# Every other hand-ordered step does one weight operation instead of two, and steps 1 to 5 have fewer filler matmuls

## The chip, the cores and the metric

The kernel runs on one core of a Trainium2 chip. The metric is the device time of one launch in microseconds (us). The engines are TensorE (PE in the rows; PEld is its weight load, which overlaps it), VectorE (DVE), ScalarE (ACT), GpSimd (POOL) and SyncE (SP, which issues most of the DMAs).

## What is computed

Two stages in float32, for 4 batches, 8 heads of 64, 768 positions, 512 model columns and 1024 inner columns:

```python
# attention: a local window of 96 keys and 8 global ones, with a slope per head
scores = q @ k.T / sqrt(64) - slope[h] * dist       # only kept keys
a = softmax(scores); x = a @ v                      # x: 768 x 512 per batch
# then a gated feed-forward layer
h = relu(x @ w_in)
c = conv_w[0]*h[t-1] + conv_w[1]*h[t] + conv_w[2]*h[t+1]
out = (h * sigmoid(c)) @ w_out
```

The weights `w_in` and `w_out` arrive as float64. They have to be brought to float32 on the core, and each is kept as two planes, a rounded high part and a low part, so that three matmuls of a faster type (high by high, high by low, low by high) give one product of float32 quality.

## The kernel before, in words

The work is cut into 8 units of 384 rows (half a batch each). Each unit has four jobs (a pair of heads each), and each job three steps of 128 rows: 96 steps in all, numbered s = 0 to 95 through the kernel. In one step TensorE multiplies scores for two heads (`scores`, L363, tile `s`), VectorE adds the distance table and takes the maxima (`maxima`, L390, two instructions, one for each head, each followed by a short read of its result), ScalarE takes exponentials into `pbuf` (`exps`, L407), TensorE transposes these (`transposes`, L432 and L434, tile `t`), ScalarE copies the result out (L437, tile `pt`), and TensorE multiplies by the values (`block`, L483, tile `pv` or `spare`). There are two score tiles in PSUM: the scores of step s can start when the exponentials of step s - 2 have read theirs. After three steps of a job its output is scaled and split into a high and a low part (`xh`, `xl`). The feed-forward layer of a unit follows: `mm1` (L521, or L542 where a slice is done early), `conv` (L567 on POOL, L568 and L569 on VectorE), gates, and `mm2` (L632).

The weights come in 16 pieces (`wr`, one DMA each, four buffers). Each piece needs four operations on VectorE and one on POOL: mask and shift (L292), sign bits (L294), low bits (L296), then POOL's copy to the high plane (L301), then the subtraction that gives the low plane (L307). That makes 64 weight operations on VectorE; eight pieces are for `w_in`, and the first four of them are all that the first half of `mm1` needs. The buffer of a piece is free for the next load after L296.

The first 14 steps are ordered by hand (`by_hand`): each engine gets its instructions in the order in which the code writes them. A step writes the scores of s, the values of s - 2, a slice of `mm1` if its weights were done early enough (`mm1_early`), a number of filler matmuls (`warm`, L152, 128x128 bf16 on zeros, into columns that nobody reads; the number stands in the table `WARM` at place s + 1), the transposes of s - 1, then the maxima and exponentials of s, and after them VectorE's other work, at the end of which stand the weight operations. A list `chores["dve"]` holds these in their order; each call of `work("dve", 0.1)` takes the next one from it. From step 14 on a scheduler places what the code hands it. There, 1.2 us of weight operations (by the program's own costs, as 0.62 for most) are handed over behind the maxima of each step until the list is empty, and each step also gets a share of `mm1`. `mm1` calls `need`, which emits any weight operation that is still missing ahead of it.

Of the kernel before, what the change touches and what calls it, by code (L numbers as in the profile page):

```python
# [40 lines left out]
HAND = 14  # L41
FREE = 4
NATIVE = 12
WARM = (64, 0, 20, 20, 16, 10, 8, 6, 6, 6, 6, 6, 6, 6, 6)
EARLY = 1
HINT = 48
DECODE_LATER = (1.2, 1.2)
# [20 lines left out]
def fast_path(tc, io):  # L68
# [81 lines left out]
    def warm(n):  # L150
        for _ in range(n):
            T.matmul(wp[:, TB:], wz, wz, start=True, stop=True)  # L152

    warm(WARM[0])

# [47 lines left out]
    def table(h, c0=0, c1=NT, X=V):  # L203
        r = slice(c0, c1)
        X.tensor_scalar(tab[:, h, r], rel[:, r], -(2.0 ** (2 - h)), 1.0, ALU.mult, ALU.mult)
# [142 lines left out]
    def free(s):  # L348
        return s < NB * FREE

    def scores(s):
        m, i = steps[s]
        b, u, hp = jobs[m]
        w = NKC[u]
        first = u == 0 and i == 0
        n = W0 if first else WIN
        k0 = key_start(u, i)
        both = ps_s.tile([P, 2, 256], F32, tag="s", name=f"s{s}")
        sp = [both[:, 0], both[:, 1]]
        for j in range(2):  # L360
            if m < NATIVE:
                rq, rk = raw[m]
                last_mm[s] = T.matmul(  # L363
                    sp[j][:, :n],
                    rq[:D, j * TB + i * P : j * TB + (i + 1) * P],
                    rk[:D, j * w + k0 : j * w + k0 + n],
                    start=True,
                    stop=True,
                )
                continue  # L370
            qh, ql, kk = qk[m]
            for n_, (q_, st, sp_) in enumerate(((qh, True, False), (ql, False, True))):
                last_mm[s] = T.matmul(  # L373
                    sp[j][:, :n],
                    q_[:, j * TB + i * P : j * TB + (i + 1) * P],
                    kk[:, j * w + k0 : j * w + k0 + n],
                    start=st,
                    stop=sp_,
                )
        st_s[s] = (sp, n, first)  # L380

    def maxima(s):
        m, i = steps[s]
        b, u, hp = jobs[m]
        sp, n, first = st_s[s]
        mm = p1.tile([P, 8], F32, tag="mm", name=f"mm{s}", bufs=6)
        for j in range(2):
            h = 2 * hp + j
            tb = tab[:, h, WIN:] if first else tab[:, h, 0:WIN]
            last_ttr[s] = V.tensor_tensor_reduce(  # L390
                out=sp[j][:, :n], in0=sp[j][:, :n], in1=tb,
                scale=-0.125, scalar=3.0e38, op0=ALU.add, op1=ALU.min,
                accum_out=mm[:, j : j + 1],
            )
        st_s[s] = (sp, n, mm)

    def exps(s):
        m, i = steps[s]
        sp, n, mm = st_s[s]
        pb = pbuf[s % NPB]  # L400
        total = mm[:, 2:4]
        if free(s):
            if i == 0:
                sums[m] = p1.tile([P, 4 * NB], F32, tag="sum", name=f"sum{m}", bufs=2)
            total = sums[m][:, 2 * i : 2 * i + 2]
        for j in range(2):
            last_exp[s] = A.activation(  # L407
                pb[:, j * WIN : j * WIN + n], sp[j][:, :n], AF.Exp,
                bias=mm[:, j : j + 1], scale=-1.0, accum_out=total[:, j : j + 1],
            )  # L410
        st_s[s] = (pb, n, mm)
        if s < SHARED and not free(s):
            A.activation(mm[:, 4:6], mm[:, 2:4], AF.Identity, bias=eps)

    def normalise(s):
        pb, n, mm = st_s[s]
        if s >= SHARED:
            V.tensor_scalar(mm[:, 4:6], mm[:, 2:4], 1.0e-9, None, ALU.add)
        V.reciprocal(mm[:, 6:8], mm[:, 4:6])  # L419
        for j in range(2):  # L420
            x, inv = pb[:, j * WIN : j * WIN + n], mm[:, 6 + j : 7 + j]
            if j and s < SHARED:
                A.activation(x, x, AF.Copy, scale=inv)
            else:
                G.tensor_scalar(x, x, inv, 1.0, ALU.mult, ALU.mult)  # L425

    def transposes(s):
        m, i = steps[s]
        pb, n, _ = st_s.pop(s)
        pt = ps_t.tile([P, 2, 2, P], F32, tag="t", name=f"t{s}")  # L430
        for j in range(2):
            T.transpose(pt[:, 0, j], pb[:, j * WIN : j * WIN + P], ident)  # L432
            if n > P:
                T.transpose(pt[:, 1, j], pb[:, j * WIN + P : j * WIN + 256], ident)  # L434
        sb = p2.tile([P, 2, 2, P], F32, tag="pt", name=f"pt{s}", bufs=NPT)
        k = 2 if n > P else 1
        last_ev[s] = A.activation(sb[:, :k], pt[:, :k], AF.Copy)  # L437
        st_pt[s] = sb
# [10 lines left out]
    def inverses(m):  # L449
        t, n = sums[m], 2 * NB  # L450
        V.tensor_scalar(t[:, n:], t[:, :n], 1.0e-9, None, ALU.add)
        V.reciprocal(t[:, n:], t[:, n:])

    def spread(m):
        for i in range(NB):
            for j in range(2):
                k = 2 * (NB + i) + j
                T.matmul(  # L458
                    wp[64 * j : 64 * j + 64, i * P : (i + 1) * P],
                    sums[m][:, k : k + 1].to_broadcast([P, D]),  # L460
                    ident, start=True, stop=True,
                )

    def factors(m):
        sums[m] = p1.tile([P, TB], F32, tag="ob", name=f"x{m}")
        A.activation(sums[m], wp[:, :TB], AF.Copy)

    def scaled(m):
        t = sums[m]
        V.tensor_tensor(t, pv[m], t, ALU.mult)  # L470
        pv[m] = t

    def block(m, i):
        if m not in pv:
            if m % 2:
                pv[m] = spare[:, :TB]
            else:
                pv[m] = ps_v.tile([P, TB], F32, tag="v", name=f"pv{m}")
        sb = st_pt.pop(NB * m + i)
        whole = jobs[m][1] == 0 and i == 0  # L480
        for c, n, q in ((0, P, 0),) if whole else ((0, P, 0), (1, NLATE, NEAR)):
            for j in range(2):
                T.matmul(  # L483
                    pv[m][64 * j : 64 * j + 64, i * P + q : (i + 1) * P],
                    vt[m][:n, i, c, 64 * j : 64 * j + 64],
                    sb[:n, c, j, q:],
                    start=c == 0,
                    stop=c == 1 or whole,
                )

    def mixed_high(m):
        xh = px.tile([P, TB], F32R, tag="xh", name=f"xh{m}")
        xl = px.tile([P, TB], F32R, tag="xl", name=f"xl{m}")
        xt[m] = (xh, xl)
        A.activation(xh, pv[m], AF.Copy)

    def mixed_low(m):
        xh, xl = xt[m]
        cur["mixed"] = V.tensor_tensor(xl, pv[m], xh.bitcast(F32), ALU.subtract)
# [5 lines left out]
    def ends(s):  # L505
        return s >= 0 and s % NB == NB - 1
# [42 lines left out]
    def mm1_early(s):  # L549
        k = begun[0]  # L550
        if k < NK - 1 and s >= 6 + NB * k and done.get((k, 0), s) < s - 1:
            for f in range(EARLY):
                mm1_slice(f, k)
            begun[0] += 1
# [167 lines left out]
    def work(eng, budget):  # L722
        q = chores[eng]
        while q and budget > 0 and q[0][0] <= cur["s"]:
            _, cost, fn, args = q.pop(0)
            fn(*args)
            budget -= cost
# [39 lines left out]
    def by_hand(s):  # L767
        m, i = steps[s]
        p, q = s - 1, s - 2
        scores(s)  # L770
        if q >= 0 and free(q):
            block(*steps[q])
        if ends(q):
            spread(q // NB)
        mm1_early(s)
        warm(WARM[s + 1])
        if ends(q):
            factors(q // NB)
        if p >= 0 and free(p):
            transposes(p)  # L780
        maxima(s)
        exps(s)
        if ends(s - 3):
            mixed_low((s - 3) // NB)
        if ends(p):
            inverses(p // NB)
        if ends(q):
            scaled(q // NB)
            mixed_high(q // NB)
        if p >= 0 and not free(p):  # L790
            normalise(p)
        if i == 0 and m + 1 < NPAIR:
            table(2 * m + 2, X=G)
            table(2 * m + 3, X=G)
        for _ in range(2 if s else 1):
            work("dve", 0.1)
        if s == HAND - 1:
            mixed_low(q // NB)
        if s == 5:
            limits()  # L800
        if s in (4, 6):
            conv_weights((s - 4) // 2)
        work("pool", 1.3)
# [276 lines left out]
```

## Time and profile before

| | |
|---|---|
| median of 3 runs | 448.04 us (446.02 to 448.59) |
| the profiled execution | 445.51 us, of which the span (first to last instruction) is 443.5 us |
| TensorE busy | 435.4 us, 98% of the span; its weight loads 378.0 us |
| VectorE, ScalarE, POOL busy | 349.3, 296.2, 208.4 us |
| DMA | 58.69 MB, 132 GB/s on average |

A busy TensorE is not a TensorE at its peak: the ends of matmuls are modelled, and neighbours overlap in the rows. The starts of neighbours tell more than the durations. The granted clock (PEclk) is 1.00 where TensorE runs at 2.4 GHz, and 0.50 at 1.2 GHz.

In the profiled execution the hand-ordered steps run from 6.6 us to 42.4 us, and the weight operations end at about 89 us. The scores of steps 14, 20, 24, 28 and 31 start at 42.36, 62.00, 74.73, 86.01 and 95.22 us.

### The profile page before, as it was taken

How to read it: one execution, taken by the hardware profiler on the slowest of the kernel's cores; microseconds unless marked ns; L12 is line 12 of the kernel's file. 1: busy time of each engine (PE TensorE's matmuls, PEld its weight loads, DVE VectorE, ACT ScalarE, POOL GpSimd, SP SyncE). 2: the span in 40 equal slices, each digit the busy share in tenths (PEclk: the TensorE clock that was granted, in tenths of full speed). 3: DMA queues.
4: the chain of work that ended last, by engine and by line, in shares of the span. 5: the costliest groups of instructions: out<-in, count | busy, mean ns of one | idle time of the engine just before them, and what ended most of it. 6: DMA issues, size and time to landing. Idle time of an engine off the chain costs nothing.

```text
span 443.5 us, 8969 instructions
## 1 busy us (share of the span) xinstructions
PE 435.4 (98%) x3044; PEld 378.0 (85%) x3044; DVE 349.3 (79%) x921; ACT 296.2 (67%) x819; POOL 208.4 (47%) x292
## 2 busy tenths in 40 slices
PE   9999999899999999999999999999999999999996
PEld 8777877689889998889989998889989998799885
DVE  5797998969989988757989898857989976657600
ACT  3566689897998775656676776656776787756511
POOL 4211644525744964546656874556656741013000
PEclk9999999999999999999999999999999999999999
DMA  7966855223144334243235334353334424970111
GB/s 216 311 205 191 251 165 168 73 84 91 64 142 143 109 109 132 77 142 117 91 133 149 105 108 126 96 138 112 108 118 141 130 85 129 333 253 0 47 50 52
DMA packets 20836, 58.69 MB, mean 132 GB/s; under 512 B 2736, under 2 KB 2992, under 8 KB 20784
## 3 DMA queue, kind: packets, MB, share of 16 engines
q1 hardware_dynamic: 16960, 51.56, 37.7%
q10 hardware_dynamic: 3824, 6.49, 4.0%
q8 instruction: 26, 0.43, 0.4%
q14 instruction: 26, 0.21, 0.1%
HBM read 51.75 MB, written 6.29 MB: 131 GB/s over the span
## 4 chain that ended last, share of the span: by engine, by line
PE 94%; DVE 3%; ACT 2%; issue 0%; POOL 0%; ACTq 0%; POOLq 0%; DVEq 0%
PE h L521 30%; PE o L632 29%; PE pv L483 8%; PE s L373 6%; PE s L363 5%; PE t L432 5%; PE t L434 4%; PE warm L152 3%; PE o L896 1%; ACT pt L437 1%; PE h L542 1%; PE spare L483 1%; PE warm L458 1%; DVE s L390 1%; DVE w L294 0%; ACT pbuf L407 0%
## 5 line engine op out<-in xcount | busy, mean ns | idle before, releaser
L425 POOL TENSOR_SCALAR pbuf<-pbuf,mm 128x232 f32<-128x232 f32 (+1 forms) x140 | 99.5, 720 | 77.8 <-DVE mm L419 58.5
L407 ACT ACTIVATE pbuf<-s,mm 128x232 f32<-128x232 f32 (+1 forms) x192 | 82.9, 441 | 45.7 <-DVE mm L390 39.3
L390 DVE CUSTOM_DVE_ANT_0 s<-s,tab 128x232 f32<-128x232 f32 (+1 forms) x192 | 73.1, 384 | 14.1 <-PE s L373 5.9
L567 POOL TENSOR_SCALAR c<-hbuf,cw 128x382 f32<-128x382 f32 (+1 forms) x64 | 49.2, 771 | 63.1 <-ACT hbuf L531 58.7
L632 PE MATMUL o<-woh,gh 128*128 128x512 f32 x184 | 75.3, 409 | 0.0
L632 PE MATMUL o<-wol,gh 128*128 128x512 f32 x184 | 73.3, 398 | 0.0
L632 PE MATMUL o<-woh,gl 128*128 128x512 f32 x184 | 72.9, 397 | 0.0
L437 ACT ACTIVATE pt<-t 128x512 f32<-128x512 f32 (+1 forms) x96 | 54.1, 564 | 18.3 <-PE t L434 16.7
L521 PE MATMUL h<-xh,wih 128*128 128x384 f32 x252 | 59.6, 349 | 0.0
L521 PE MATMUL h<-xl,wih 128*128 128x384 f32 x252 | 58.0, 343 | 0.0
L521 PE MATMUL h<-xh,wil 128*128 128x384 f32 x252 | 56.7, 345 | 0.0
L568 DVE SCALAR_TENSOR_TENSOR c<-hbuf,cw,c 128x382 f32<-128x382 f32 (+1 forms) x64 | 47.6, 750 | 10.5 <-POOL c L567 10.2
L432 PE MATMUL t<-ident,pbuf 128*128 128x128 f32 x192 | 46.4, 276 | 0.2
L521 PEld LDWEIGHTS h<-xh,wih 128*128 128x128 f32 x252 | 43.4, 190 | 3.2 <-issue 1.7
L521 PEld LDWEIGHTS h<-xh,wil 128*128 128x128 f32 x252 | 44.1, 190 | 2.0 <-issue 1.5
L521 PEld LDWEIGHTS h<-xl,wih 128*128 128x128 f32 x252 | 43.2, 189 | 1.3 <-issue 0.9
L569 DVE SCALAR_TENSOR_TENSOR c<-hbuf,cw,c 128x382 f32<-128x382 f32 (+1 forms) x64 | 43.8, 687 | 0.5
L483 PEld LDWEIGHTS pv<-pt,v 128*64 128x64 f32 (+1 forms) x664 | 34.0, 136 | 10.1 <-issue 4.1
L483 PE MATMUL pv<-pt,v 128*64 128x128 f32 (+1 forms) x664 | 40.9, 268 | 0.9 <-ACT pt L437 0.7
L632 PEld LDWEIGHTS o<-woh,gl 128*128 128x128 f32 x184 | 34.6, 188 | 7.8
L632 PEld LDWEIGHTS o<-wol,gh 128*128 128x128 f32 x184 | 34.7, 189 | 6.3
L632 PEld LDWEIGHTS o<-woh,gh 128*128 128x128 f32 x184 | 34.7, 189 | 6.3
(123 smaller groups left out, 856.4 us busy)
## 6 DMA issues: line engine op xcount, KB each, us to landing
v<-in_vv SPq DMA_DIRECT2D x32, 384.0 KB, 3.8
wr<-in_w SPq DMA_DIRECT2D x16, 512.0 KB, 4.8
check<-in_w SPq DMA_DIRECT2D x16, 512.0 KB, 4.4
rq<-in_qk SPq DMA_DIRECT2D x20, 384.0 KB, 3.2
rk<-in_qk SPq DMA_DIRECT2D x12, 504.0 KB, 3.7
out<-ob ACTq DMA_DIRECT2D x23, 256.0 KB, 2.5
rk<-in_qk SPq DMA_DIRECT2D x8, 400.0 KB, 3.3
rq<-in_qk SPq DMA_DIRECT2D x11, 192.0 KB, 5.4
```

The lines of the kernel that those rows point to most:

```text
L373: last_mm[s] = T.matmul(sp[j][:, :n], q_[:, j * TB + i * P : j * TB + (i + 1) * P], kk[:, j * w + k0 : j * w + k0 + n], start=st, stop=sp_,)
L390: last_ttr[s] = V.tensor_tensor_reduce(out=sp[j][:, :n], in0=sp[j][:, :n], in1=tb, scale=-0.125, scalar=3.0e38, op0=ALU.add, op1=ALU.min, ...
L407: last_exp[s] = A.activation(pb[:, j * WIN : j * WIN + n], sp[j][:, :n], AF.Exp, bias=mm[:, j : j + 1], scale=-1.0, accum_out=total[:, j : ...
L425: G.tensor_scalar(x, x, inv, 1.0, ALU.mult, ALU.mult)
L432: T.transpose(pt[:, 0, j], pb[:, j * WIN : j * WIN + P], ident)
L437: last_ev[s] = A.activation(sb[:, :k], pt[:, :k], AF.Copy)
L483: T.matmul(pv[m][64 * j : 64 * j + 64, i * P + q : (i + 1) * P], vt[m][:n, i, c, 64 * j : 64 * j + 64], sb[:n, c, j, q:], start=c == 0, st ...
L521: T.matmul(ps[:, :TB], w_[:, k, fs], x_, start=part == 0 and k == 0, stop=part == 2 and k == NK - 1,)
L567: G.tensor_scalar(c, *tap(1), 1.0, ALU.mult, ALU.mult)
L568: V.scalar_tensor_tensor(c, *tap(0), c, ALU.mult, ALU.add)
L569: V.scalar_tensor_tensor(c, *tap(2), c, ALU.mult, ALU.add)
L632: T.matmul(ps, g_[:, f], w_[:, f], start=f == 0 and part == 0, stop=f == NF - 1 and part == 2,)
```

## The change

Two lines change. The table `WARM` has 12, 10, 8, 8 and 6 fillers behind the scores of steps 1 to 5, where it had 20, 20, 16, 10 and 8. In the hand-ordered steps the loop over `work("dve", 0.1)` runs once in odd steps and twice in even ones (and once in step 0, as before, where the list is still empty).

```diff
-WARM = (64, 0, 20, 20, 16, 10, 8, 6, 6, 6, 6, 6, 6, 6, 6)
+WARM = (64, 0, 12, 10, 8, 8, 6, 6, 6, 6, 6, 6, 6, 6, 6)
...
-        for _ in range(2 if s else 1):
+        for _ in range(2 - s % 2 if s else 1):
             work("dve", 0.1)
```

On VectorE in steps 1 to 3 (names end in the piece or the step: `s2` are the scores of step 2, `w0_0` is piece 0), before:

```order
L292 TENSOR_SCALAR w0_0_278<-wr0_0_228 128x512
L294 SCALAR_TENSOR_TENSOR w0_0_278<-wr0_0_228,w0_0_278 128x512
L390 ISA s2_281,mm2_314<-s2_281,tab_182 128x232
L390 ISA mm2_314 128x1
L390 ISA s2_281,mm2_314<-s2_281,tab_182 128x232
L390 ISA mm2_314 128x1
L296 SCALAR_TENSOR_TENSOR w0_0_278<-wr0_0_228,w0_0_278 128x512
L292 TENSOR_SCALAR w1_0_322<-wr1_0_232 128x512
```

and in the changed kernel:

```order
L292 TENSOR_SCALAR w0_0_270<-wr0_0_228 128x512
L390 ISA s2_272,mm2_295<-s2_272,tab_182 128x232
L390 ISA mm2_295 128x1
L390 ISA s2_272,mm2_295<-s2_272,tab_182 128x232
L390 ISA mm2_295 128x1
L294 SCALAR_TENSOR_TENSOR w0_0_270<-wr0_0_228,w0_0_270 128x512
L296 SCALAR_TENSOR_TENSOR w0_0_270<-wr0_0_228,w0_0_270 128x512
```

One operation stands between the maxima of steps 1 and 2 where there were two. Over steps 1 to 13 there were 26 weight operations (7 of L292, 7 of L294, 6 of L296, 6 of L307) and there are 19 (5, 5, 5, 4).

On TensorE in step 6 (`h0_0` is the early slice of `mm1`, `xh0` and `xl0` the output of the first job, `t5` the transposes of step 5), before, with the six fillers that follow left out:

```order
L363 MATMUL s6_455<-rk2_234,rq2_235 128x128 x2
L483 MATMUL spare_97<-pt4_438,v1_240 64x128 x2
L483 MATMUL spare_97<-pt4_438,v1_240 64x104 x2
L542 MATMUL h0_0_462<-xh0_410,wih_202 128x384
L542 MATMUL h0_0_462<-xl0_411,wih_202 128x384
L542 MATMUL h0_0_462<-xh0_410,wil_203 128x384
```

and in step 7 of the changed kernel, behind its scores:

```order
L483 MATMUL spare_97<-pt5_439,v1_240 64x128 x2
L483 MATMUL spare_97<-pt5_439,v1_240 64x104 x2
L458 MATMUL warm_96<-ident_169,sum1_330 64x128 x6
L542 MATMUL h0_0_473<-xh0_377,wih_202 128x384
L542 MATMUL h0_0_473<-xl0_378,wih_202 128x384
L542 MATMUL h0_0_473<-xh0_377,wil_203 128x384
```

The slice waits for the low plane of the first piece, which is done later; so it stands in step 7 and not in step 6. The third slice moves in the same way from step 12 to step 13; the second stays in step 9.

On VectorE at the end of the weight operations (`w7_1` is the last piece, `c0` a conv), before:

```order
L390 ISA s28_1291,mm28_1294<-s28_1291,tab_182 128x232
L390 ISA mm28_1294 128x1
L419 RECIPROCAL mm26_1232<-mm26_1232 128x2
L419 RECIPROCAL mm27_1264<-mm27_1264 128x2
L307 TENSOR_TENSOR wol_205<-w7_1_1226,woh_204 128x512
L390 ISA s28_1291,mm28_1294<-s28_1291,tab_182 128x232
```

and in the changed kernel:

```order
L390 ISA s29_1302,mm29_1305<-s29_1302,tab_182 128x232
L390 ISA mm29_1305 128x1
L419 RECIPROCAL mm28_1260<-mm28_1260 128x2
L307 TENSOR_TENSOR wol_205<-w7_1_1247,woh_204 128x512
L568 SCALAR_TENSOR_TENSOR c0_755<-hbuf_206,cw_201,c0_755 128x382
L419 RECIPROCAL mm29_1305<-mm29_1305 128x2
```

The last weight operation stood between the two maxima of step 28, and stands behind those of step 29. From about step 51 on the order on TensorE is the same in both.

## Rows read from the trace of the kernel before

**Rows 1.** The page, part 1: engine, busy us (share of span), instructions.

```profile
PE 435.4 (98%) x3044; PEld 378.0 (85%) x3044; DVE 349.3 (79%) x921; ACT 296.2 (67%) x819; POOL 208.4 (47%) x292
```

**Rows 2.** Busy time by stretch; the first line names the columns.

```profile
core 0: us, PE busy (x) PEld busy (x) DVE busy (x) ACT busy (x) POOL busy (x), PEclk, DMA share, GB/s
6.00:42.40 36.40, 36.07 (x368) 27.73 (x365) 30.72 (x108) 20.52 (x72) 9.27 (x26) 1.00 0.79 244
42.40:64.00 21.60, 21.60 (x130) 17.63 (x130) 20.60 (x58) 16.37 (x51) 11.72 (x15) 1.00 0.78 232
64.00:86.00 22.00, 19.21 (x134) 14.43 (x132) 20.63 (x68) 18.92 (x62) 10.33 (x16) 1.00 0.42 131
86.00:90.00 4.00, 3.99 (x14) 3.31 (x14) 3.79 (x11) 3.44 (x14) 2.72 (x4) 0.62 0.00 0
90.00:98.00 8.00, 8.00 (x61) 6.62 (x61) 3.95 (x18) 7.26 (x24) 1.72 (x3) 0.98 0.40 116
98.00:443.50 345.50, 341.52 (x2292) 303.28 (x2290) 266.94 (x652) 228.40 (x599) 170.96 (x218) 1.00 0.36 117
```

**Rows 3.** TensorE's waits, 42 to 98 us: total us, times, longest.

```profile
PE s L363 <- ACT pbuf L407: 1.9, 3, 1.0
PE pv L483 <- ACT pt L437: 0.7, 1, 0.7
```

**Rows 4.** TensorE's timeline: start us, us, what (out<-in, shape, count), idle before.

```profile
8.00 1.29 PE L152 MATMUL warm<-setup 128*128 128x128 bf16 x20
9.12 0.39 PE L432 MATMUL t<-ident,pbuf 128*128 128x128 f32 x2
...
10.79 1.29 PE L152 MATMUL warm<-setup 128*128 128x128 bf16 x20
...
12.46 0.71 PE L363 MATMUL s<-rk,rq 64*128 64x128 f32 x4
...
20.62 0.71 PE L363 MATMUL s<-rk,rq 64*128 64x128 f32 x4
...
21.99 0.44 PE L542 MATMUL h<-xh,wih 128*128 128x384 f32 x1
...
22.97 0.28 PE L432 MATMUL t<-ident,pbuf 128*128 128x128 f32 x1
...
26.36 1.05 PE L363 MATMUL s<-rk,rq 64*128 64x232 f32 x4
```

**Rows 5.** ScalarE's timeline, exponentials of steps 0 and 5.

```profile
8.46 0.36 ACT L407 ACTIVATE pbuf<-s,mm 128x128 f32<-128x128 f32 x1
...
21.60 0.45 ACT L407 ACTIVATE pbuf<-s,mm 128x232 f32<-128x232 f32 x1 [0.21 <-DVE mm L390]
```

**Rows 6.** Weight operations on VectorE, 9 to 43 us: busy us, mean ns.

```profile
L294 DVE SCALAR_TENSOR_TENSOR w<-wr,w 128x512 int32<-128x512 int32 x6 | 4.3, 718 | 0.0
L296 DVE SCALAR_TENSOR_TENSOR w<-wr,w 128x512 int32<-128x512 int32 x6 | 4.1, 682 | 0.1
...
L307 DVE TENSOR_TENSOR wil<-w,wih 128x512 fp32r<-128x512 f32 x5 | 3.4, 684 | 0.0
L292 DVE TENSOR_SCALAR w<-wr 128x512 int32<-128x512 int32 x7 | 3.1, 441 | 0.0
```

**Rows 7.** VectorE's waits, 89 to 98 us: total us, times, longest.

```profile
DVE s L390 <- PE s L363: 2.9, 2, 1.5
DVE s L390 <- ACT xh L495: 1.1, 1, 1.1
```

**Rows 8.** TensorE's timeline, scores of steps 28 and 31.

```profile
86.01 1.05 PE L363 MATMUL s<-rk,rq 64*128 64x232 f32 x4 [1.04 <-ACT pbuf L407]
...
95.22 1.05 PE L363 MATMUL s<-rk,rq 64*128 64x232 f32 x4
```

**Rows 9.** Timeline of VectorE and POOL around 59 us.

```profile
58.92 1.04 DVE L307 TENSOR_TENSOR wol<-w,woh 128x512 fp32r<-128x512 f32 x1
59.37 1.06 POOL L301 CAST woh<-w 128x512 fp32r<-128x512 f32 x1
```

## Prediction

> **What bounds the kernel now.** I read the page's busy shares first. TensorE is busy for 98% of the span, no other engine for over 79% [rows 1], so the question is where TensorE can give time back and where it waits. The busy times by stretch answer that [rows 2]. Up to 64 us TensorE has no gap worth naming (0.33 us in the 36.4 us from 6 us on). From 64 to 86 us it lacks 2.8 us (22.00 less 19.21) while VectorE is busy for 20.6 of the 22. Then comes a stretch from 86 to 90 us at a granted clock of 0.62, a mix of the two levels 2.4 and 1.2 GHz. Behind 98 us it lacks 4.0 of 345.5 us. The waits of TensorE say what it lacked from 64 us on: the scores waited 1.9 us in three places for ScalarE's exponentials to free a score tile, and the values 0.7 us for a transposed tile [rows 3]. The exponentials wait for the maxima, and the maxima stand in VectorE's line behind the weight operations. So there are three regimes: hand-ordered steps, dense on TensorE; a stretch up to about 90 us in which VectorE's weight operations set the pace; and the rest, dense on TensorE, in which nothing of this change stands.
>
> **The fillers.** Step 1 has 20 fillers between 8.00 and 9.12 us, step 2 starts 20 at 10.79 [rows 4]; that is 1.12 / 20 = 56 ns each. The change takes away 8 + 10 + 8 + 2 + 2 = 30, so 1.7 us at most, if TensorE has other work ready each time. Step by step:
> - Step 1: 8 x 56 = 0.45 us less, but the transposes of step 0 need its exponentials, which end at 8.46 + 0.36 = 8.82 [rows 5]. They can start at about 8.87, not 9.12: 0.25 us earlier.
> - Steps 2 and 3: 0.56 and 0.45 us; the exponentials that their transposes need are out by then, since VectorE now has one weight operation ahead of the maxima of step 2. Lead 1.26 us.
> - Steps 4 and 5: 0.11 us each. Lead 1.48 us at the scores of step 6.
> - Step 6 loses its slice of `mm1`, which takes 22.97 - 21.99 less six fillers of 0.056, 0.64 us [rows 4]. TensorE would reach the transposes of step 5 at 22.97 - 1.48 - 0.64 = 20.85. Their exponentials started at 21.60, straight behind the maxima [rows 5]; they gain about the 1.37 us of steps 1 to 4 and lose 0.27, because the two weight operations ahead of them are the dearer L294 and L296 and not L292 and L307 (718 + 682 - 441 - 684 ns [rows 6]). That is 20.5, and two of 0.45 end at 21.4. TensorE waits 0.6 us there, and the slice comes on top in step 7. Lead from step 8 on: 1.48 - 0.6 = 0.9 us.
>
> So I take a lead of 0.9 us, with 0 and 1.7 as ends. The steps behind, with their six fillers, are dense at a granted clock of 1.00 [rows 2], so steps 1 to 5 with 6 to 12 fillers should hold the clock; that costs nothing.
>
> **The weight operations.** Seven of the 26 leave the first 14 steps: two each of L292, L294 and L307, one L296: 2 x 0.44 + 2 x 0.72 + 2 x 0.68 + 0.68 = 4.4 us [rows 6]. In the first 42 us TensorE was dense, so taking them away there buys nothing but the cover above. They come back where VectorE is full: the new order has all 64 done ahead of the maxima of step 30, as the old one had. In between it catches up gradually. Behind the maxima of step 16 up to those of step 26 it has 31 weight operations where there were 28, so three more, at 0.63 us on average [rows 6] 1.9 us; up to step 28 it has 36 for 32; up to step 30 it has 39 for 32.
> The place where this meets TensorE is the scores of step 28 at 86.01 us, which already waited 1.04 us for the exponentials of step 26 [rows 8]. They move by 1.9 - 0.9 = +1.0 us if VectorE has no slack. It had some: 22.00 - 20.63 = 1.4 us from 64 to 86 us [rows 2], part of it TensorE's own lateness, and an engine with work at hand fills such gaps. If all of it is filled, the shift is -0.4. I take the middle, +0.3.
> Behind that the debt is paid: at step 30 VectorE owes 4.4 - 0.9 = 3.5 us, and it waited 2.9 + 1.1 = 4.0 us between 89 and 98 us for scores and a copy [rows 7]. So I charge nothing after step 31; without this slack the cost would be up to 3.5 us more, and the scores of step 31 at 95.22 us [rows 8] would show it.
>
> VectorE's operations may be dearer in their new place. The one that ran beside POOL's copy at 59 us took 1.04 us [rows 9], where five of its kind in the first 43 us took 0.68 [rows 6]; POOL is busy for 11.72 of 21.60 us from 42 us on, and for 9.27 of 36.40 before [rows 2]. Between 0 and 7 x 0.36 = 2.5 us; I take 0.2, since an operation meets a copy rarely.
> The Trainium skill, page "SBUF — State Buffer", section "Who interferes with whom", says that a VectorE instruction with two inputs in SBUF and a GpSimd instruction that reads SBUF exclude each other, and that the later one waits until the other is done. The trace agrees in this one place; by that rule the loss is what is left of a copy each time, and the upper end of 2.5 us would be the price, which is a rival below.
>
> **The DMAs.** The loads of weight pieces stand in SP's line and wait for a buffer that L296 frees. With L296 later, loads behind them in that line could be late. In the new order the queries and keys of the fourth job stand ahead of the second such load, not behind it; the values of the same job and what follows stand behind the third, which waits for step 8 and not for step 6. The job needs these values at step 11, three steps later, so I cost this at nothing; if the cover fails, the values of step 9 are late and TensorE stands in step 11.
>
> **The slow stretch.** From 86 to 90 us the clock was 0.62 and from 90 to 98 us 0.98: 4 x 0.38 + 8 x 0.02 = 1.7 us lost [rows 2], right behind the gap at 86 us. As the gap stays, I expect the stretch to stay: 0.
>
> **Sum.** The shift at the scores of step 28 is +0.3 with the lead in it, and the dearer operations add 0.2: +0.5. On the profiled execution (445.51 us, its span 443.5 us and 2.0 us around it) this is 446.0 us; that execution is 2.5 us under the median of 448.04 us, and on the median it is 448.5 us. That is no change that a measurement can tell: 0.5% is 2.2 us.
>
> **Rivals.**
> - *The lead is kept and VectorE's gaps swallow the debt.* If nothing is lost in steps 1 and 6, the lead is 1.7; with all 1.4 us of VectorE's gaps filled the shift at step 28 is 1.9 - 1.4 - 1.7 = -1.2, and with a shorter gap on TensorE half of the slow stretch may go too (-0.85). That gives -2.1, 446.0 us. For it: the gaps of VectorE are real. Against it: the waits in steps 1 and 6 follow from rows.
> - *Slower: the stall before step 28 gets long enough for the clock to fall twice.* TensorE reaches this stretch 0.9 us earlier and leaves it 1.0 us later, so it stands for 2.8 + 1.9 = 4.7 us in it, not 2.8. If the clock falls once more, that is another 1.7 us where TensorE is no longer covered: +1.0 + 1.7 = +2.7, 450.7 us. It decides from the point where a second gap of about the 1.04 us of step 28 appears. For it: the clock fell behind a gap this short. Against it: a slow TensorE inside the stretch is partly hidden, since VectorE is late there anyway.
> - *The fillers only covered waits.* The lead is 0, TensorE idles where they stood, and the shift is 1.9 less half of 1.4, +1.2: 449.2 us. Against it: the transposes of steps 2 to 5 follow their fillers without a gap.
>
> - *The moved operations meet POOL's copies every time.* Then 2.5 us come on top of +0.3, 450.8 us. For it: the one pair of rows at 59 us. Against it: POOL is idle for nearly half of that stretch.
>
> **Chances.** Forecast 0.43, first rival 0.2, second 0.18, third 0.14, fourth 0.05. The forecast lies within 0.5%; of the first rival about half crosses the bound (0.1), of the second and fourth nearly all (0.18), of the third a third (0.05). With 0.03 for what I have not thought of on the fast side that is faster 0.13, same 0.64, slower 0.23. The range goes from just under the first rival to the second: 445.7 to 450.7; the likeliest case by itself spans 447.3 to 449.7.
>
> **What would show it.** The scores of step 6 start at 19.1 us (20.62 before), those of step 8 at 25.5 (26.36) with a gap of 0.6 us on TensorE ahead of the transposes of step 5; VectorE has gaps in the odd steps; the scores of step 28 start between 85.5 and 87 us, those of step 31 within 1 us of 95.2; one slow stretch near 86 to 91 us. The forecast is wrong if step 14 starts later than 42.3 us or earlier than 40.7, if step 31 starts more than 2 us away from 95.2, or if the clock falls before 60 us.

## The result, and the profile after

| | before | after |
|---|---|---|
| median, 20 executions each | 446.00 us (445.15 to 449.42) | 448.92 us (445.39 to 450.67) |
| ratio, 95% interval | 1 | 1.0052 (1.0033 to 1.0070) |
| the profiled execution, its span | 445.51, 443.5 us | 448.59, 446.6 us |
| first scores start at | 6.57 us | 7.30 us |

The change makes the kernel slower by about half a per cent. (The ratio comes from all executions, whose means are 446.67 us in before and 448.98 in after, so it is not the ratio of the medians.) The median of before from 20 executions lies 2 us under the one from three on which the forecast stood. One thing has to be known to read all times here: the executions of before fall into two groups, about 445.3 to 446.4 us at a mean granted clock of 0.994 or more and 447.6 to 449.6 us mostly at 0.992 or less, and its median moves with their mix (446.0, 445.9, 446.1 and 447.3 us in four batches). Of the changed kernel's executions 31 of 32 (with those of an experiment below) had 0.992 or less.

The first scores start 0.73 us later in this profile. They stand behind the 64 fillers with which `WARM` opens, which are the same in both kernels. From 5.0 to 6.5 us 29 of these ran in before and 17 in after; between 1 and 5 us it was 38 in both, about 105 ns each where later ones take 56. All 64, first before, then after:

```profile
0.99 5.65 PE L152 MATMUL warm<-setup 128*128 128x128 bf16 x64 [0.99 <-POOL setup L141]
```

```profile
0.99 6.37 PE L152 MATMUL warm<-setup 128*128 128x128 bf16 x64 [0.99 <-POOL setup L141]
```

Over the profiles of all kernels here the first scores start between 6.19 and 7.47 us (7.30 and 7.14 us in two of the changed kernel), and no run tells whether the change has a part in that. So places are compared below by their distance from the first scores. Part 1 of the page of after, and its busy times by stretch:

```profile
PE 437.1 (98%) x3014; PEld 377.9 (85%) x3014; DVE 349.9 (78%) x921; ACT 296.1 (66%) x819; POOL 214.3 (48%) x292
```

```profile
core 0: us, PE busy (x) PEld busy (x) DVE busy (x) ACT busy (x) POOL busy (x), PEclk, DMA share, GB/s
6.00:42.40 36.40, 35.44 (x341) 26.74 (x340) 27.80 (x101) 20.19 (x72) 8.72 (x25) 1.00 0.72 224
42.40:64.00 21.60, 21.60 (x135) 17.45 (x132) 20.17 (x56) 16.25 (x51) 10.99 (x14) 1.00 0.73 218
64.00:86.00 22.00, 19.48 (x136) 14.77 (x134) 22.00 (x68) 18.58 (x58) 13.70 (x16) 1.00 0.60 179
86.00:90.00 4.00, 2.86 (x10) 2.18 (x10) 4.00 (x11) 3.51 (x15) 2.33 (x3) 0.81 0.00 0
90.00:98.00 8.00, 8.00 (x49) 6.24 (x48) 5.86 (x20) 6.21 (x20) 3.24 (x6) 0.67 0.26 75
98.00:446.60 348.60, 344.68 (x2308) 305.53 (x2307) 267.25 (x659) 230.10 (x605) 173.73 (x218) 1.00 0.36 116
```

TensorE has 30 matmuls fewer and yet 1.7 us more of busy time than in [rows 1]: something made matmuls longer. The column PEclk says what. From 90 to 98 us the clock was 0.67, where [rows 2] has 0.98. And VectorE, which had 1.4 us of gaps from 64 to 86 us [rows 2], has none: 22.00 of 22.00.

The waits of TensorE from 42 to 98 us (total us, times, longest) have grown little against [rows 3], 1.9 to 2.5 us for the scores:

```profile
PE s L363 <- ACT pbuf L407: 2.5, 4, 1.3
PE pv L483 <- ACT pt L437: 0.7, 1, 0.7
PE t L432 <- ACT pt L437: 0.3, 1, 0.3
```

The clock in short stretches, first before, then after:

```profile
86.00:87.00 1.00, 0.99 (x5) 0.69 (x5) 1.00 (x2) 1.00 (x5) 1.00 (x2) 0.97 0.00 0
87.00:88.00 1.00, 1.00 (x4) 1.00 (x4) 0.96 (x3) 0.96 (x5) 0.58 (x1) 0.50 0.00 0
...
89.00:90.00 1.00, 1.00 (x5) 0.65 (x3) 0.82 (x4) 0.70 (x4) 0.70 (x2) 0.50 0.00 0
90.00:91.00 1.00, 1.00 (x5) 0.80 (x4) 0.00 (x0) 1.00 (x5) 0.04 (x1) 0.82 0.08 16
```

```profile
88.00:89.00 1.00, 1.00 (x5) 0.88 (x5) 1.00 (x4) 0.85 (x3) 0.72 (x1) 0.73 0.00 0
89.00:92.00 3.00, 3.00 (x9) 1.89 (x7) 3.00 (x11) 1.90 (x7) 1.57 (x3) 0.50 0.00 0
92.00:95.00 3.00, 3.00 (x12) 2.67 (x12) 2.41 (x8) 2.89 (x11) 1.92 (x3) 0.50 0.56 172
95.00:96.00 1.00, 1.00 (x18) 0.81 (x18) 0.16 (x1) 0.11 (x1) 0.00 (x0) 0.86 0.00 0
```

Before lost 0.03 + 3 x 0.50 + 0.18 = 1.7 us of full clock in one stretch at 1.2 GHz, after 0.27 + 6 x 0.50 + 0.14 = 3.4 us: the stretch is twice as long. It begins behind the stall ahead of step 28, as in before. TensorE's timeline of after around it (start, us, what, idle before; the scores of steps 27, 28, 29 and 31):

```profile
84.22 0.71 PE L363 MATMUL s<-rk,rq 64*128 64x128 f32 x4 [0.37 <-ACT pbuf L407]
...
87.14 1.05 PE L363 MATMUL s<-rk,rq 64*128 64x232 f32 x4 [1.32 <-ACT pbuf L407]
...
90.07 1.91 PE L363 MATMUL s<-rk,rq 64*128 64x232 f32 x4
...
97.94 1.05 PE L363 MATMUL s<-rk,rq 64*128 64x232 f32 x4
```

From the first scores step 28 is at 87.14 - 7.30 = 79.84 us (before 86.01 - 6.57 = 79.44 [rows 8], so +0.40) and step 31 at 90.64 (before 88.65, +1.99). From about 178 us on the distance is constant, +2.43 us. With the 0.73 us by which the first scores came later, that is the 3.1 us between the two spans.

### The profile page after: what moved, and what is told of

The parts are those of the page before. It is cut to its first block, busy times and chain, and to the rows that moved or that the text cites. A ratio compares the mean times of both kernels' runs of the same rounds, so it can differ in the third digit from the quotient of the medians.

```text
span 446.6 us, 8913 instructions
## 1 busy us (share of the span) xinstructions
PE 437.1 (98%) x3014; PEld 377.9 (85%) x3014; DVE 349.9 (78%) x921; ACT 296.1 (66%) x819; POOL 214.3 (48%) x292
## 4 chain that ended last, share of the span: by engine, by line
PE 89%; DVE 6%; ACT 3%; issue 1%; POOL 0%; ACTq 0%; POOLq 0%
PE o L632 29%; PE h L521 28%; PE pv L483 8%; PE s L373 6%; PE s L363 5%; PE t L432 4%; PE t L434 4%; PE warm L152 3%; PE o L896 1%; DVE s L390 1%; ACT pbuf L407 1%; DVE c L568 1%; ACT pt L437 1%; DVE w L294 1%; DVE w L296 1%; DVE c L569 1%
## 5 line engine op out<-in xcount | busy, mean ns | idle before, releaser
L425 POOL TENSOR_SCALAR pbuf<-pbuf,mm 128x232 f32<-128x232 f32 (+1 forms) x140 | 104.3, 754 | 83.4 <-DVE mm L419 64.1
L407 ACT ACTIVATE pbuf<-s,mm 128x232 f32<-128x232 f32 (+1 forms) x192 | 82.6, 439 | 50.1 <-DVE mm L390 42.3
L567 POOL TENSOR_SCALAR c<-hbuf,cw 128x382 f32<-128x382 f32 (+1 forms) x64 | 51.9, 814 | 56.0 <-ACT hbuf L531 52.8
L568 DVE SCALAR_TENSOR_TENSOR c<-hbuf,cw,c 128x382 f32<-128x382 f32 (+1 forms) x64 | 47.6, 748 | 10.9 <-POOL c L567 10.7
L432 PE MATMUL t<-ident,pbuf 128*128 128x128 f32 x192 | 47.3, 278 | 0.6 <-ACT pt L437 0.3
L434 PE MATMUL t<-ident,pbuf 128*128 128x128 f32 x160 | 39.9, 276 | 0.1
```

Of the source, the lines that this page charges most:

```text
L407: last_exp[s] = A.activation(pb[:, j * WIN : j * WIN + n], sp[j][:, :n], AF.Exp, bias=mm[:, j : j + 1], scale=-1.0, accum_out=total[:, j : ...
L567: G.tensor_scalar(c, *tap(1), 1.0, ALU.mult, ALU.mult)
L568: V.scalar_tensor_tensor(c, *tap(0), c, ALU.mult, ALU.add)
```

## The experiments

In the table, "step 28" is the distance of its scores from the first scores, "stall" the idle time ahead of it, "clock" the granted clock from 86 to 98 us, all of the profiled execution; "low" counts executions at a mean clock of 0.992 or less. The batches of before had the medians 445.91 (experiments 1 to 4), 446.08 (5 to 8) and 447.34 us (9 to 11), and each ratio is against before in its own batch. Experiments 9 to 11 ran on another chip than 1 to 8.

| | median us | ratio (95%) | step 28 | stall | clock | low |
|---|---|---|---|---|---|---|
| before | 446.00 | 1 | 79.44 | 1.04 | 0.86 | 6 of 23, 9 of 34, 13 of 26 in the three batches |
| after | 448.92 | 1.0052 (1.0033 to 1.0070) | 79.84 | 1.32 | 0.72 | 19 of 20 |
| 1 fillers alone | 444.83 | 0.9991 (0.9962 to 1.0019) | 78.01 | 1.04 | 1.00 | 4 of 12 |
| 2 weight operations alone | 449.87 | 1.0092 (1.0075 to 1.0108) | 82.31 | 1.32 | 0.72 | 5 of 6 |
| 3 after, stall filled | 448.04 | 1.0043 (1.0030 to 1.0056) | 79.91 | 0.21 | 1.00 | 0 of 6 |
| 4 before, stall filled | 446.47 | 1.0002 (0.9982 to 1.0022) | 79.72 | 0.20 | 1.00 | 0 of 11 |
| 5 after again | 448.89 | 1.0053 (1.0028 to 1.0077) | 79.86 | 1.32 | 0.72 | 12 of 12 |
| 6 three deferred | 445.25 | 0.9977 (0.9949 to 1.0005) | 78.06 | 1.04 | 1.00 | 2 of 12 |
| 7 four deferred, late steps | 443.97 | 0.9937 (0.9915 to 0.9959) | 77.18 | 0.70 | 1.00 | 0 of 12 |
| 8 fillers alone, stall filled | 445.23 | 0.9972 (0.9945 to 0.9999) | 78.02 | 0.20 | 1.00 | 0 of 12 |
| 9 as 7, old fillers | 445.15 | 0.9959 (0.9936 to 0.9981) | 78.64 | 0.68 | 1.00 | 0 of 12 |
| 10 after, less work per planned step | 445.12 | 0.9944 (0.9922 to 0.9967) | 77.91 | 0.79 just ahead | 1.00 | 0 of 9 |
| 11 five deferred | 444.47 | 0.9944 (0.9916 to 0.9972) | 78.18 | 1.04 | 1.00 | 4 of 12 |

### 1 and 2: each part alone

```diff
 experiment 1: after's WARM in before
-WARM = (64, 0, 20, 20, 16, 10, 8, 6, 6, 6, 6, 6, 6, 6, 6)
+WARM = (64, 0, 12, 10, 8, 8, 6, 6, 6, 6, 6, 6, 6, 6, 6)
 experiment 2: after's loop in before
-        for _ in range(2 if s else 1):
+        for _ in range(2 - s % 2 if s else 1):
```

> The fillers of steps 1 to 5 are cut as in the change, but every step does two weight operations, as before. Theory A (the loss comes from the weight operations that move behind step 14; they lengthen TensorE's stall before the scores of step 28, and that doubles the stretch at half clock): the early slice of mm1 stays in step 6, the lead of 1.0 to 1.5 us at step 8 is kept up to step 28, one slow stretch of about 3.4 us stays: 0.996 to 0.999 of the kernel before. Theory B (the fewer fillers themselves make the clock fall, or the opening slow): as slow as the changed kernel, 1.004 to 1.007. Theory C (the difference is where runs happen to start): 1.000.

> All fillers as before; odd steps do one weight operation. Theory A: the debt of seven weight operations without any lead, so the stall before step 28 is longer than in the changed kernel and the slow stretch is the long one (about 7 us): 1.006 to 1.010 of the kernel before. Theory B: 1.000. Theory C: 1.000.

The fillers alone bring the lead and it holds (step 8 at 18.34 us from the first scores, before 19.79; step 28 at 78.01); in the profile 1.87 us are left of it at the end, by the medians nothing that the interval can tell. The weight operations alone cost 0.9%. The slow stretch that theory A left standing is not in this profile, and four of twelve executions were low. In the profiles the two add up to about the whole (-1.87 and +4.56 us against +2.43 from the first scores on), so the fillers are not what costs. In experiment 2 the scores of step 28 stood behind the same stall as in after, not a longer one as expected, and 2.47 us later than in after (88.50 - 6.19 = 82.31), more than the lead of 1.45 us that the fillers bring:

```profile
88.50 1.05 PE L363 MATMUL s<-rk,rq 64*128 64x232 f32 x4 [1.32 <-ACT pbuf L407]
```

Against before, step 28 is 2.87 us late there, and 2.05 us of that stood at step 14, before the deferred operations came due, with waits of TensorE for ScalarE of 0.33, 0.18 and 0.64 us ahead of it.

### 3 and 4: the stall filled

```diff
 experiment 3 in after, experiment 4 in before
+KEEP = {(0, 7, 1): 20}      # behind these first matmuls, ahead of step 28
+    wk = const.tile([P, 96], BF16, name="wk")
+    G.memset(wk, 0.0)
+        for _ in range(KEEP.get((n, f, part), 0)):
+            T.matmul(ps[:96, :P], wk, ident.bitcast(BF16)[:, :P], start=False, stop=False)
```

> The changed kernel with 20 more matmuls (56 ns each, zeros added into a tile of mm1) in the place where TensorE stands idle before the scores of step 28; nothing else is moved ahead of that place. Theory A: TensorE is busy in the stall, the clock does not fall (mean granted clock 1.00) and about 3.4 us of half clock go, which is 3.4 us: 0.996 to 1.000 of the kernel before. Theory D (the late VectorE is the loss, and the slow clock costs nothing because TensorE would wait anyway): 1.004 to 1.007, as the changed kernel.

> The kernel before with the same 20 matmuls in the same place. Theory A: its slow stretch of about 3.4 us goes, 1.7 us less: 0.995 to 0.998. Theory D: 1.000 to 1.003 (the 20 matmuls take 1.1 us where TensorE stands for 1.0).

The granted clock was 1.00 from 86 to 98 us in both. TensorE's timeline of experiment 4 shows the 20 matmuls inside the stall (the last two rows are steps 28 and 29). From step 28 to step 29 it took 2.66 us, where before took 4.05 (86.01 to 90.06):

```profile
84.31 1.28 PE L529 MATMUL h<-ident,wk 128*96 128x128 bf16 x20
...
86.02 1.05 PE L366 MATMUL s<-rk,rq 64*128 64x232 f32 x4 [0.20 <-ACT pbuf L410]
...
88.68 1.05 PE L366 MATMUL s<-rk,rq 64*128 64x232 f32 x4
```

But nothing of it reached the end: 446.47 us, a ratio of 1.0002, which lies in theory D's range. The added instructions changed the order that the planner makes of everything behind (about 30 places on TensorE), and new waits stand there, all between 118 and 140 us, where before waits for nothing from 98 us on (waits of TensorE, experiment 4, 98 to 180 us):

```profile
PE s L376 <- ACT pbuf L410: 0.5, 2, 0.3
PE t L437 <- ACT pbuf L426: 0.5, 1, 0.5
```

In after, the same matmuls gave back 0.9 us by the medians, not the 3.4 us expected, and the ratio of 1.0043 lies in theory D's range too. The trace of experiment 3 shows where the rest went. These are its scores of steps 28 and 31, two waits behind them, and one near its end:

```profile
87.16 1.05 PE L366 MATMUL s<-rk,rq 64*128 64x232 f32 x4 [0.21 <-ACT pbuf L410]
...
95.72 1.05 PE L366 MATMUL s<-rk,rq 64*128 64x232 f32 x4 [0.48 <-ACT pbuf L410]
...
131.84 0.30 PE L435 MATMUL t<-ident,pbuf 128*128 128x128 f32 x1 [0.27 <-ACT pt L440]
132.62 0.38 PE L376 MATMUL s<-kk,qh 128*128 128x232 f32 x1 [0.47 <-ACT pbuf L410]
...
398.87 1.59 PE L524 MATMUL h<-xh,wih 128*128 128x384 f32 x4 [1.83 <-ACT hbuf L536]
```

Step 28 is where after has it (79.91 us from the first scores). Step 31 is at 95.72 - 7.25 = 88.47 us, where after has 90.64, and TensorE has done the same work by then (20 matmuls and three transposes more). So the slow stretch cost after 2.17 us in this place. From about 178 us on experiment 3 is 1.00 us behind before, where after is 2.43 behind: 1.43 of the 2.17 us are kept, and the other 0.74 are the two waits at 132 us, which after does not have. So the size that theory A gave (3.4 us) was too high, and the new order hid a third of what was there. The profiled execution is also the slowest of the six (450.94 us): behind the wait of 1.83 us the clock fell once more (0.66 on average from 398 to 403 us), which no other profile here shows.

### 5 to 8: more executions, and parts of the deferral

```diff
 experiment 5: after, unchanged
 experiment 6: one operation in steps 1, 3 and 5 alone
+        for _ in range(2 - (s % 2 if s < 7 else 0) if s else 1):
 experiment 7: one operation in steps 7, 9, 11 and 13 alone
+        for _ in range(2 - (s % 2 if s > 6 else 0) if s else 1):
 experiment 8: experiment 1 with KEEP of experiment 4
```

> The changed kernel, unchanged, for more executions. Theory A (the change costs through TensorE's clock alone, by the second half of the half-clock stretch at 89 to 95 us): the one execution so far at a mean clock of 1.000 took 445.39 us, as before does, so every execution with a mean clock of 0.998 or more comes out at 445.0 to 446.2, those at 0.992 at 448.2 to 449.2. Rival D (VectorE, late by the deferred weight operations, costs the time itself): executions at a clock of 0.998 or more still take 447 us or more, and 445.39 was a chance. Median by both 448.5 to 449.3.

No execution of experiment 5 had a clock above 0.992, so its test could not be made. What stands is the one execution of after at 1.000, 445.39 us, against 448.19 to 450.67 us for the other 19: the same program, 2.8 us apart or more. Against it stands one execution of experiment 2 at 0.996, which took 450.24 us, no less than those at 0.992 or less.

> After, but only steps 1, 3 and 5 do one weight operation; from step 7 on two again (three operations deferred, 1.9 us, in place of seven, 4.4 us). Theory A with the deferred work as the cause of the longer stall: VectorE reaches the maxima before step 28 no later than in before, one half-clock stretch of 3.4 us or none, median 444.8 to 446.0. Rival E (the early weight operations' new place, which delayed the slice of the first matmuls to step 7 and took the lead at step 8 from 1.45 to 0.39 us, is the cause): lead at step 8 stays at about 0.4 us and the stretch stays about 6.9 us, median 448 to 449.

> After, but only steps 7, 9, 11 and 13 do one weight operation; steps 1 to 5 do two as before (four operations deferred, 2.5 us). Theory A with the deferred work as the cause: lead at step 8 back at 1.4 us, but the stall before step 28 as long as in after and a half-clock stretch of 5 to 7 us, median 446.5 to 448.5. Rival E (the early place is the cause): as with the fillers alone, lead 1.4 us held, median 444.2 to 445.2.

Both were faster than after by 3.7 and 5.0 us. In experiment 6 step 8 is at 19.65 us, a lead of only 0.14 us and so less than after's, and still step 28 comes at 78.06. So with three operations deferred the lead lost in the hand-ordered steps (rival E) is not what decides at step 28. It is the operations of steps 1, 3 and 5 that lose it: step 14 starts 35.66 us from the first scores in experiment 6, 34.33 in experiment 7 and 34.38 with the fillers alone. For experiment 7 both theories missed in part: the lead at step 8 is 1.46 us as both said, but neither a long stall nor a slow stretch came, and it was faster than either gave. TensorE's timeline ahead of step 28, experiments 6 and 7:

```profile
84.74 1.05 PE L363 MATMUL s<-rk,rq 64*128 64x232 f32 x4 [1.04 <-ACT pbuf L407]
```

```profile
84.56 1.05 PE L363 MATMUL s<-rk,rq 64*128 64x232 f32 x4 [0.70 <-ACT pbuf L407]
```

> The fillers' part of the change alone, and 20 small matmuls that add zeros behind the first matmuls ahead of step 28, in the stall there. Theory A: the upper group of the fillers-only executions (447.1 to 449.0 at a clock of 0.989 to 0.992) is gone, all executions at 0.998 or more, median 444.0 to 445.0. Rival D: the 20 matmuls move later instructions in the order, as they did in before, and that costs about 0.7 us again: median 445.0 to 446.0, still without the upper group.

The low executions are gone, as expected, and the median of 445.23 us lies in the range of rival D, not of theory A, with three executions of 446.9 to 447.4 us at full clock that stay unexplained.

### 9 to 11: VectorE's load

```diff
 experiment 9: experiment 7 with before's WARM
 experiment 10: after with
-DECODE_LATER = (1.2, 1.2)
+DECODE_LATER = (0.9, 0.9)
 experiment 11: one operation in steps 5, 7, 9, 11 and 13 alone
+        for _ in range(2 - (s % 2 if s > 4 else 0) if s else 1):
```

> Steps 7, 9, 11 and 13 do one weight operation, the other steps two, and the fillers of before (20, 20, 16, 10, 8). Theory F (the late half of the operations costs nothing and the fillers give the gain): what is gained with both, 2.0 us, splits into the fillers' lead, about 1.4 us, and the end of the half-clock stretch; so 445.0 to 446.2 here, at a clock of 0.998 or more if the stretch goes, 0.994 if not. Rival G (the late deferral itself gives the gain): 444.0 to 444.7, as with both. Rival H (deferral costs without the fillers' lead, as all seven operations did): 447 or more.

> After, with the budget of weight work per planned step cut from 1.2 to 0.9 (the first weight pieces end at step 34 of the steps, not 30): TensorE's order and the hand-ordered steps stay, VectorE has less to do between 42 and 86 us. Theory I (after is late at step 28, and the clock halves for twice as long, because VectorE is busy without a gap from 64 to 86 us with the seven deferred operations): gaps come back there, step 28 about 1.5 us sooner after the first scores (78.0 to 78.8 in place of 79.84), no stretch at half clock or one of 3.4 us, median 444.5 to 446.5 unless the weights come too late for the second matmuls. Rival J (the delay was made in the hand-ordered steps and stays): step 28 at 79.5 or later, median 448 or more.

> After, but steps 1 and 3 do two weight operations: five deferred (3.1 us) in place of seven, between the four of the best variant (443.97 us) and after (448.89 us). Theory I (a limit that VectorE's work before step 28 passes): VectorE full from 64 to 86 us, a longer half-clock stretch in some executions, two groups of times, median 444.2 to 447. If the early lead decided instead (the slice of the first matmuls moves with step 5's operation, lead at step 8 about 0.4 us): as after, 448 to 449.

Experiment 9 fell where theory F put it; the fillers' part in experiment 7 is then 1.2 us, taken across two chips. Experiment 10 is the test of VectorE: all seven operations are deferred, the steps up to 15 start within 0.02 us of after's, and only the work per planned step is less. Step 28 came 1.93 us sooner than in after (77.91), the clock stayed at 1.00, and the median fell by 3.8 us. VectorE's busy time ahead of step 28 (the fifth column, in two stretches) in after, in experiment 10 and in experiment 7:

```profile
64.00:75.00 11.00, 9.81 (x70) 7.46 (x68) 11.00 (x34) 9.23 (x30) 6.87 (x8) 1.00 0.74 220
75.00:86.00 11.00, 9.67 (x66) 7.31 (x66) 11.00 (x35) 9.35 (x30) 6.83 (x8) 1.00 0.47 138
```

```profile
64.00:75.00 11.00, 10.49 (x73) 8.56 (x73) 10.93 (x34) 9.24 (x29) 7.46 (x9) 1.00 0.63 205
75.00:86.00 11.00, 10.21 (x73) 8.15 (x73) 10.92 (x35) 10.16 (x37) 7.45 (x9) 1.00 0.70 201
```

```profile
64.00:75.00 11.00, 10.02 (x68) 7.60 (x69) 10.45 (x33) 9.81 (x31) 5.74 (x8) 1.00 0.59 187
75.00:86.00 11.00, 10.01 (x68) 7.71 (x68) 10.96 (x35) 10.30 (x38) 5.88 (x9) 1.00 0.40 118
```

VectorE's gaps in experiment 10 are only 0.15 us, less than expected, and yet TensorE got 20.70 us of work done in the 22 against 19.48: a full VectorE alone does not make the loss. What goes with it is the number of weight operations that stand between the maxima of step 14 and those of step 26, behind which the score tile of step 28 comes free. It is 34 in before and 37 in after and experiment 2; 33 to 35 in experiments 6, 7, 9 and 11, which have fewer to make up; and 29 in experiment 10. The stall at the scores became a wait of the transposes for POOL just ahead:

```profile
85.12 0.33 PE L432 MATMUL t<-ident,pbuf 128*128 128x128 f32 x1 [0.79 <-POOL pbuf L425]
85.38 1.05 PE L363 MATMUL s<-rk,rq 64*128 64x232 f32 x4
```

The expectation of 10 said that TensorE's order would stay. It does in the hand-ordered steps only; behind them the planner made another order (50 places), so this run changes VectorE's load and the order with it. Experiment 11 came out in the expected range, with two groups (eight executions of 443.4 to 444.6 us, four of 446.1 to 448.0 us at 0.992 or less). It kept its lead (1.44 us at step 8), so the rival that it names, in which the slice of `mm1` moves, was not put to the test.

## Why the prediction was right or wrong

The time, 448.92 us, lies 0.4 us beside the forecast of 448.5 and in its range, but in part by luck: the forecast stood on a median of before that was 2 us too high. What it said of the change, +0.5 us, was too little: it was +2.4 us from the first scores on, and +2.9 by the medians. By the prediction's own signs the forecast was wrong: step 14 starts at 42.71 us, where later than 42.3 was to speak against it, and step 31 at 97.94 us, 2.7 us from 95.2. Of both, 0.73 us is the later start of the first scores.

- *The fillers.* Step 6 starts at 19.90 - 7.30 = 12.60 us from the first scores, before at 14.05 [rows 4]: a lead of 1.45 us, predicted 1.48. Right. The waits that follow are the miss (TensorE of after; the first row is step 6, the last step 8):

```profile
19.90 0.71 PE L363 MATMUL s<-rk,rq 64*128 64x128 f32 x4
21.05 0.62 PE L483 MATMUL spare<-pt,v 128*64 128x128 f32 x8 [0.45 <-ACT pt L437]
...
22.30 0.33 PE L432 MATMUL t<-ident,pbuf 128*128 128x128 f32 x1 [0.19 <-ACT pbuf L407]
22.74 0.33 PE L434 MATMUL t<-ident,pbuf 128*128 128x128 f32 x1
...
26.70 1.05 PE L363 MATMUL s<-rk,rq 64*128 64x232 f32 x4
```

Step 6 took 3.31 us to step 7 (23.21), in before 2.89, and lacks a slice of 0.64 us: 1.06 us of waits, where 0.6 was predicted. Step 7 took 0.64 us longer with the slice, as predicted. So the lead at step 8 is 1.45 - 0.42 - 0.64 = 0.39 us, not 0.9. The gap of 0.6 was predicted ahead of the transposes of step 5, and there it is: 0.19 us, and 0.3 us more between the first two (0.44 us from start to start, in before 0.12). The 0.45 us ahead of the spare matmuls were not foreseen: a small activation of ScalarE (L236) waited for VectorE's two dearer operations, and the eviction of a transposed tile stood behind it (ScalarE of after):

```profile
20.20 0.31 ACT L236 ACTIVATE setup<-setup,misc 128x24 int32<-128x24 int32 x1 [0.54 <-DVE cw L237]
20.42 0.58 ACT L437 ACTIVATE pt<-t 128x512 f32<-128x512 f32 x1
```

In experiment 6 this slip decided nothing at step 28. With all seven operations deferred a lead did count: after is ahead of experiment 2 by 2.43 us at step 14 and by 2.47 at step 28.

- *The weight operations.* The shift at step 28 was predicted as +0.3 (-0.4 to +1.0) and is +0.40. The size is right in part by luck: the lead to start from was 0.38 us at step 14, not 0.9, and from there to step 28 after lost 0.78 us, not 1.2, so two misses nearly cancel. That VectorE would fill its gaps was right, 22.00 of 22.00. No run measures the debt's price of 1.9 us by itself. Against experiment 1, which has the same fillers and defers nothing, step 28 comes 1.83 us later in after, but 1.03 us of that stood at step 14 already.
- *Dearer operations.* +0.2 was charged. VectorE's weight operations from 42 to 90 us had means of 725, 710, 734, 692 and 511 ns in five groups, where before had 722, 698, 727, 686 and 476; with after's counts (11, 10, 6, 5, 11) that is 0.6 us more. Nothing was charged for the other operations, and more was lost there: VectorE's conv (L568, seven in either kernel) took 792 ns on average for 700, and POOL's (L567, seven) 1104 for 758, which is 2.4 us of POOL's time. No run tells what made them longer. The Trainium skill, page "SBUF — State Buffer", section "Who interferes with whom", says that a VectorE instruction with two inputs in SBUF and a GpSimd instruction that reads SBUF exclude each other. Of the 2.5 us that the fourth rival charged for this, the weight operations in the trace of after show a quarter. The row at 59 us [rows 9] was also misread. When that L307 began, POOL was at a conv, and its copy began only at 59.37 us, so the 0.36 us stood beside the conv (before):

```profile
58.83 0.59 POOL L567 TENSOR_SCALAR c<-hbuf,cw 128x382 f32<-128x382 f32 x1 [1.35 <-ACT hbuf L531]
```

- *The DMAs.* Nothing was charged, and that was right: up to 43 us TensorE waits for ScalarE twice in after, and for no load.
- *The slow stretch.* "As the gap stays, I expect the stretch to stay: 0." This is the step that failed, a term put at nothing. The gap did stay, and grew by 0.28 us to 1.32; the stretch doubled, 1.7 us of lost clock to 3.4. Between steps 28 and 31 after fell back by 1.99 - 0.40 = 1.6 us, and with the stall filled all of it is gone at step 31 (experiment 3: 88.47 us, before 88.65). That is near the second rival, "slower: the stall before step 28 gets long enough for the clock to fall twice". Its place and its price held: it gave +2.7 us, and +2.4 were measured, with 1.6 us for its 1.7, and its shift at step 28 (+1.0) too high. Its sign did not: no second gap of about 1.04 us appeared (0.37 and 1.32 us ahead of steps 27 and 28), and the clock fell once and stayed at 1.2 GHz for 6.8 us, where it was 3.4 us before.
- *Behind step 31* nothing was charged, and 0.4 us more were lost by 178 us; after that nothing.

What the runs show: the weight operations cost and the fillers don't (1, 2); not the deferral as such costs, since three, four or five operations can be deferred at no loss (6, 7, 9, 11); and with seven deferred the loss goes when VectorE has less weight work between the hand-ordered steps and step 28 (10). How the loss divides between late VectorE and slow TensorE is shown up to step 31: there the slow stretch is 2.17 us, more than the 1.99 us that after had lost against before, which has a slow stretch itself. What stays open is how much of that lasts to the end in after's own order. The single execution of after at full clock (445.39 us) says all of it; experiment 3 kept 1.43 us in its profile and 0.9 us by the medians, in another order with two more waits. With the stall filled in both, after and before are 0.26 us apart from about 178 us on (experiments 3 and 4, +1.00 and +0.74 us against before) and 1.6 us by the medians. A test that holds the clock and the order behind step 28 at once was not made.

The best version is experiment 7, new fillers and one operation in steps 7, 9, 11 and 13 alone: 443.97 us, 0.6% under before and 1.1% under after.

## What to carry to other kernels

Work that is deferred from a stretch where its engine has time comes due where that engine sets the pace, and it is the amount due before the next late wait that decides: with four operations deferred the work due before step 28 was as before and the kernel gained, with seven it was three operations more and the kernel lost. A stall that already stands beside a fall of the clock should be priced with the next fall as well, since 0.3 us more of waiting went with another 3.4 us at half clock, or 1.7 us of lost clock. Where a planner orders what follows, every added instruction is also another order: compare such kernels by their waits, and don't read the end time as the price of the added instruction. In experiment 3 the place where the instructions were added told more (2.17 us at step 31) than the end time (0.9 us).

## What the runs showed of the hardware

The mean clock goes with the stall ahead of step 28, over all kernels here whose stall wasn't filled: with 1.32 us (after, experiments 2 and 5) 36 of 38 executions were at 0.992 or less; with 1.04 us (experiments 1, 6, 11) 10 of 36, and before, with the same stall, 28 of 83 in three batches; with 0.70 us and less (7, 9) none of 24. The stall is that of the profiled execution of each kernel, the clock that of every execution. This is what was seen beside the stall, not a limit: the kernels also differ in what TensorE did ahead of it.

A slow stretch of 3.4 us cost before nothing that the executions show: two of 34 in one batch had a mean clock of 1.000 and took 445.81 and 446.29 us, and of the 23 with 0.994 to 0.996 all but two took 445.4 to 446.4. In its place the stretch did cost: from step 28 to step 29 before took 4.05 us, and 2.66 with the stall filled and the clock at 1.00 (experiment 4). Experiment 1, whose profile has no slow stretch, shows how this gets lost behind: its lead on before rises from 1.43 us at step 28 to 2.95 at step 31 and is 1.87 from about 178 us on. More of it showed at the end: at 0.992 and less before took 447.6 to 449.6 us.
